# Two FNet and two H3 layers on one core: the 64-row products of rows 4 to 15 in runs of six over 384 columns, on three fixed banks

## The chip, the core and the metric

The kernel runs on one NeuronCore of a Trainium2 chip. TensorE (PE in the profile) multiplies matrices and writes the products to PSUM banks; PEld is its loading of weights. VectorE (DVE) and ScalarE (ACT) work element by element, GpSimd (POOL) does a few small steps and issues some transfers, SyncE (SP) issues most of the others. Each engine takes its instructions in order. The metric is the device time of one execution in microseconds, as the median of several runs.

## The reference

x has 2048 positions of 576 channels. Two layers alternate, twice:

```
x = x + FNet(layernorm(x));  x = x + H3(layernorm(x))
FNet(x) = Cr @ (x @ Wr.T) - Ci @ (x @ Wi.T)        # real part of a 2-D Fourier transform
H3(q)   = q * (longconv(kv, ssm_k) + kv * ssm_D),  kv = shiftconv(k, shift_k) * v
```

The shift convolution has 4 taps, the long one is causal over all 2048 positions; the reference does it by a transform of length 4096. k, v and the filters are inputs and do not depend on x, so this branch can be computed at any time before the first H3 layer needs it.

## The kernel before

A matrix product in fp32 accuracy is made of three: each operand is split into a high part (ScalarE rounds it, `split`, L92) and a low part (VectorE subtracts, L93), and TensorE adds high x high, high x low and low x high in one bank.

`layer` computes the sequence transform of a FNet layer. Its steps (g, tb, k) run over the real and the imaginary matrix (g), four blocks of 512 output positions (tb) and 16 blocks of 128 positions to sum over (k). A step has 14 products of 512 columns, 12 into four banks `s` and two into the bank `rm` for the last 64 channels; the left operand is X (tile `mats`), the right a 128 x 512 block of the matrix that `load_c` loads two steps ahead and splits. These are the "sequence products" below. After each block of positions `hidden` makes the transform over channels, 27 products of 288 columns into a bank `bk`.

`branch` is a generator that computes the convolution branch between these steps; the main loop calls it a fixed number of times in each step, so the sequence products set its pace. Its first part, f1, takes the 16 rows j of the input as (position in groups of 16) and transforms each over 128 entries by two transforms of 64. `todo` lists the pieces (j, src), src 1 for the filter (kernel) and 0 for the signal: first the filters of rows 0 to 3, then their signals, then both of each row from 4 on.

- `f1_loads` loads the piece and the row's constants, `convolve` makes the shift convolution on VectorE in small steps, paced so that a row's signal is ready when its piece comes up.
- `f1_split` multiplies in v for a signal and splits the piece into one of three buffers `xf`.
- `f1_products` takes a piece of 576 columns in two halves of 288. For each half it takes two banks from `bank()` (one tag with three buffers) and makes six products: for each of the three combinations of high and low one on partitions 0 to 63 and one on 64 to 127, which use a 64-row half of TensorE each and go to different banks. ScalarE copies both banks out (L436) and issues the store to `t_d` (L437), of which there is one for each column half.
- A piece's products are made one piece after its split, from the ninth piece on (`F1_LAG`) two pieces after.

Which instruction stands where on an engine is decided by a scheduler: it keeps the dependencies and the order that `issue_after` (here the helper `behind`) demands, and is otherwise free, so that the products of f1 are laid between the sequence products, six together or fewer.

After f1 comes the middle part: it reads `t_d` in groups of four frequencies (`load_feed`, L569), transforms, multiplies filter and signal and transforms back; its products stand between later sequence products and go to `bank()` too. Then the result is gated with x, and the second half of the kernel repeats the two layers with the filters' result kept.

Of the kernel before, what the change touches and what calls it, by code (L numbers as in the profile page):

```python
# [10 lines left out]
F32 = mybir.dt.float32  # L11
FR = mybir.dt.float32r
AF = mybir.ActivationFunctionType
OP = mybir.AluOpType

P = 128
HP = P // 2
S = 2048
D = 576
J = S // P  # L20
TB = 4
NT = 512
HD = D // 2
NC = 4
# [5 lines left out]
ROWS = (0, 1, 2, 3, 4, 5, 6, 7, 8, 9)  # L30
K_FIRST = 4
F1_16 = 5
F1_LAG = 8
F1_END = 42
W_FROM = 41
HOLD = 125
# [16 lines left out]
CRAW = 2  # L53
# [6 lines left out]
SC_AT = 8 + 4 * STAT  # L60
# [5 lines left out]
def fnet_h3_kernel(ctx: ExitStack, tc: tile.TileContext, x, c_mat, w_re, w_im, k_pad, v, shift_k,  # L66
                   ssm_k, ssm_d, f1c, i2c, midc, out):
    nc = tc.nc
    cst = ctx.enter_context(tc.tile_pool(name="cst", bufs=1))
    sb = ctx.enter_context(tc.tile_pool(name="sb", bufs=1))  # L70
    psp = ctx.enter_context(tc.tile_pool(name="psp", bufs=1, space=bass.MemoryType.PSUM))
    dr = ctx.enter_context(tc.tile_pool(name="dr", bufs=1, space=bass.MemoryType.DRAM))

    def mm(ps, lhsT, rhs, first, last, more=False):
        nc.tensor.matmul(ps, lhsT, rhs, start=first, stop=last, skip_group_check=more)  # L75

    def bank():
        return psp.tile([P, NT], F32, tag="b", bufs=3, name="bk")

    acc4 = [psp.tile([P, NT], F32, tag=f"s{i}", name=f"s{i}") for i in range(4)]  # L80
    last_pair = [acc4[2:]]
# [9 lines left out]
    def split(h, l, src):  # L91
        a = nc.scalar.activation(h, src, AF.Copy).ins  # L92
        return a, nc.vector.tensor_tensor(l, src, h.bitcast(F32), OP.subtract).ins  # L93

    @contextmanager
    def behind(*instructions):
        with ExitStack() as stack:
            for i in instructions:
                stack.enter_context(tc.issue_after(i))
            yield  # L100
# [22 lines left out]
    ring = {}  # L123

    def lay(t, at, *sizes):

        for name, words, n in sizes:
            ring.setdefault(name, Ring()).tiles.extend(t[:, at + i * words:at + (i + 1) * words] for i in range(n))
            at += n * words
        assert at <= t.shape[1], (at, t.shape, sizes)  # L130
        return at
# [5 lines left out]
    def two(v):  # L137
        return v.rearrange("p (a n) -> p a n", a=2)
# [11 lines left out]
    flts = flat(FLT, F32, "flts")  # L150
# [5 lines left out]
    anchor, made, rounded, pows, biased, halved, added, evac, parted, stored = [], [], [], [], [], [], [], [], [], []  # L156
# [35 lines left out]
        made.append(nc.vector.tensor_tensor(t[:, D + REM:], y[:, :NC * P], h[:, :NC * P], OP.subtract).ins)  # L192
        return t

    t_d = [dr.tile([P, 2 * J, 2, HD], F32, name=f"t{h}") for h in range(2)]
    v_d = [dr.tile([P, J, 2, HD], F32, name=f"vd{h}") for h in range(2)]
    yb_d = [dr.tile([P, D], F32, name=f"yb{j}") for j in range(J)]
    xa_d = [dr.tile([P, D], F32, name=f"xa{j}") for j in range(J)]
# [46 lines left out]
        load_after(xs[:, ch].bitcast(F32), w_d[ch])  # L245
        W[ch] = two(xs[:, ch])

    U = {}

    def ut(ch):  # L250
        return um[0][:, ch * WIDE:(ch + 1) * WIDE].rearrange("p (a n) -> p a n", a=2)
# [42 lines left out]
    def layer(get_x, xres, done, pending, blocks=TB):  # L294
        steps = [(g, tb, k) for tb in range(blocks) for g in range(2) for k in range(J)]
        for n, (g, tb, k) in enumerate(steps):
            for i in range(2):
                if n == 0 and steps[i] not in CT:
                    load_c(steps[i])
            if n + 2 < len(steps):  # L300
                load_c(steps[n + 2])
            for i in range(XLEAD + 1 if blocks == TB else 1):
                if n + i < J:
                    get_x(n + i)
            if k == 0:
                ps = list(acc4)
                ps.append(psp.tile([P, NT], F32, tag="rm", name="rm"))
            c = CT.pop(steps[n])
            first, last = k == 0, k == J - 1
            while last and g == 0 and pending:  # L310
                yield n, None
            for dc in range(NC):
                xh = X[k][:, dc * P:(dc + 1) * P]
                xl = X[k][:, D + REM + dc * P:D + REM + (dc + 1) * P]
                mm(ps[dc], xh, c[0], first, False)
                mm(ps[dc], xh, c[1], False, False)
                mm(ps[dc], xl, c[0], False, last)
                if dc == NC // 2 - 1:
                    yield n, False
                elif blocks == TB and dc < NC - 1 and n >= MID_FROM and not last:  # L320
                    yield n, "part"
                if last:
                    (evac_u if blocks == TB else save_u)(g, ps, dc)
            xr = X[k][:, NC * P:D + REM]
            mm(ps[NC], xr, c[0], first, False)
            mm(ps[NC], xr, c[1], False, last)
            if last and blocks < TB:
                store_r(tb, g, ps[NC])
            elif last:
                evac_r(g, ps)  # L330
                if g == 1:
                    us = dict(U)
                    pending.extend([us, tb, jj, xres, done] for jj in range(TB))
            yield n, True

    def parts(i):
        v = ring[i]()
        return v[:, :D], v[:, D:]
# [3 lines left out]

    def branch():
        f1r = region_b(FR, "f1r")
        lay(f1r, 0, ("xf", 2 * D, 3), ("fc", 2 * P, 5))
        at = lay(flts, SC_AT + CRAW * NT, ("so", D, 4), ("land", D, 3))
        lay(flts, at, ("craw", NT, 1))
        f1f = region_a(F32, "f1f")
        ks = f1f[:, :KR * 2 * D]
        lay(f1f, KR * 2 * D, ("wt", 2 * D, 2), ("rp", 2 * D, 2))  # L350
        tmp = f1f[:, 8 * 2 * D:]
        wt, rows, landed, fcs = [], {}, {}, {}
        k_loaded = [0]

        def load_w4():
# [20 lines left out]
        def convolve():  # L376
            for i in range(J // 2):
                if not wt:
                    load_w4()
                load_k(i + KR - 1)  # L380
                rp = rows[i] = two(ring["rp"]())
                for t in range(4):
                    out_t = two(tmp) if t else rp
                    for n, k in k_rows(2 * i + t):
                        nc.vector.tensor_tensor(out_t[:, n], k, wt[3 - t][:, n], OP.mult)
                    yield
                    if t == 1:
                        load_k(i + KR)
                    if t:
                        nc.vector.tensor_tensor(rp, rp, out_t, OP.add)  # L390
                        yield
# [22 lines left out]
        def f1_split(j, src):  # L414
            r = landed.pop((j, src))
            if not src:
                row = rows[j // 2][:, j % 2, :]
                nc.vector.tensor_tensor(row, row, r, OP.mult)
                r = row
            elif j == 0:  # L420
                nc.vector.tensor_tensor(r[:1], r[:1], tmp[:1, D:], OP.add)
            xf = parts("xf")
            parted[:] = split(xf[0], xf[1], r)
            return xf

        def f1_products(j, src, xf, fc):
            for hf in range(2):
                so = two(ring["so"]())
                cs = slice(hf * HD, (hf + 1) * HD)
                ps = [bank() for _ in range(2)]  # L430
                for n, (a, b) in enumerate(((0, 0), (0, 1), (1, 0))):
                    for i in range(2):
                        rows = slice(i * HP, (i + 1) * HP)
                        mm(ps[i][:, :HD], fc[rows, a, :], xf[b][rows, cs], n == 0, n == 2)
                for i in range(2):
                    stored[:] = [nc.scalar.activation(so[:, i, :], ps[i][:, :HD], AF.Copy).ins]  # L436
                nc.scalar.dma_start(t_d[hf][:, j::J, src, :], so)  # L437
                yield

        conv, made_ops, split_up = convolve(), 0, []  # L440
        for n, (j, src) in enumerate(todo):
            f1_loads(n + 1)
            if n < 2:
                yield
            split_up.append((j, src, f1_split(j, src), fcs[j]))
            products = f1_products(*split_up.pop(0)) if len(split_up) > (1 if n < F1_LAG else 2) else iter(())
            if n:
                f1_loads(n + 3)
            later = [m for m in range(n + 1, len(todo)) if todo[m][1] == 0 and 7 * (todo[m][0] // 2 + 1) > made_ops]
            for half in range(2):  # L450
                next(products, 0)
                if later and n > 2:
                    left = 7 * (todo[later[0]][0] // 2 + 1) - made_ops
                    for _ in range(-(-left // (2 * (later[0] - n) - half)) if left > 0 else 0):
                        next(conv)
                        made_ops += 1
                yield
        next(conv, 0)
        for left_over in split_up:
            yield from f1_products(*left_over)  # L460
        m1 = region_b(FR, "mid")
        kk_at = SC_AT + CRAW * NT + 4 * D
        at = lay(m1, 0, ("df", 2 * D, 3), ("mc", 4 * P, 1))
# [88 lines left out]
        def load_feed(i):  # L552
            if i < len(feeds):
                kind, hf, q = feeds[i]
                landed[i] = ring["land"]()
                load_after(landed[i], v_d[hf][:, q].rearrange("p c d -> p (c d)") if kind else
                           t_d[hf][4 * q:4 * q + 4].rearrange("m j s d -> (m j) (s d)"))

        def load_fc(k):
            if k < len(rows):  # L560
# [189 lines left out]
    for n, whole in layer(get_x0, lambda j: x[:, j, :], done0, pending):  # L750
# [30 lines left out]
        m = n - PREP  # L781
# [355 lines left out]
```

## Time and profile before

| | |
|---|---|
| median of 3 runs | 1210.28 us (1209.79 to 1210.68) |
| the profiled execution | 1208.79 us |
| its span, first to last instruction | 1207.0 us |
| busy: PE, PEld, DVE | 1189.2, 1004.4, 840.7 us |
| busy: ACT, POOL | 664.1, 76.2 us |
| bytes moved | 259.85 MB, mean 215 GB/s |

Busy times are unions of the time in which an engine has an instruction at work. TensorE's matmuls are pipelined: the next starts before the one before has ended, so a busy TensorE can still go faster, and its costs are better read from one start to the next. In a row of the timeline stand the start, the duration of the merged group, the engine, the line, the tiles written and read, the shape (rows x columns of the array, then partitions x elements) and the count. In a row of the waits stand who waited, for whom, the sum in us, the number of times and the longest. In a row of a windows view stand the stretch, its length and each engine's busy time with its number of instructions, then the granted clock, the DMA engines' busy share and the rate.

### The profile page before, as it was taken

Reading aid. Unit: us, or ns where it says so; the run is one execution under the profiler, and the core shown is the slowest. Engines: PE = TensorE matmul, PEld = TensorE weight load, DVE = VectorE, ACT = ScalarE, POOL = GpSimd, SP = SyncE. Lnnn points to the kernel's source line nnn. Section 1 sums busy time; section 2 is a strip of 40 time slices with the busy share of each in tenths; the row PEclk is TensorE's granted clock in tenths of the full one; section 3 lists DMA queues with packets and bytes.
Section 4 is the critical chain, followed back from the end, with each engine's and each line's share of the span. In section 5 each row is a group of like instructions: output and inputs, shape, how many; then the busy total and the mean of one; then the engine's idle time right before and its main releaser. Section 6 shows DMA issues by size and latency. Waiting matters only on the chain.

```text
span 1207.0 us, 18256 instructions
## 1 busy us (share of the span) xinstructions
PE 1189.2 (99%) x6320; PEld 1004.4 (83%) x6320; DVE 840.7 (70%) x1498; ACT 664.1 (55%) x1335; POOL 76.2 (6%) x116
## 2 busy tenths in 40 slices
PE   8999999999999999999999999999999999999997
PEld 5776667998888888888988898888888888789997
DVE  7889983678787677775346666775766777774764
ACT  7855555578876677775345667544434445450210
POOL 2210000000000000001101111000000000001111
PEclk9999999999999999999999999999999999999999
DMA  9768877645666666547967677872672677795621
GB/s 337 271 206 282 280 240 249 211 149 164 204 195 201 226 178 204 182 147 231 323 189 236 233 246 225 279 253 83 196 279 92 194 281 269 239 322 160 219 93 40
DMA packets 146110, 259.85 MB, mean 215 GB/s; under 512 B 15841, under 2 KB 46817, under 8 KB 146018
## 3 DMA queue, kind: packets, MB, share of 16 engines
q1 hardware_dynamic: 102674, 205.45, 52.3%
q10 hardware_dynamic: 36432, 42.63, 10.3%
q0 software_dynamic: 6912, 10.62, 3.4%
q8 instruction: 49, 0.80, 0.3%
q14 instruction: 43, 0.35, 0.1%
HBM read 191.99 MB, written 66.65 MB: 214 GB/s over the span
## 4 chain that ended last, share of the span: by engine, by line
PE 72%; ACT 4%; DVE 2%; DMA 2%; issue 1%; ACTq 0%; SPq 0%; POOLq 0%; DVEq 0%
PE s L75 39%; PE bk L75 29%; PE rm L75 4%; ACT flts L490 2%; ACT mid L490 1%; DMA wd<-w 1%; DMA t<-ud 1%; DMA flts<-in_c_mat 1%; ACT mats L92 0%; ACT u L92 0%; DVE mid L496 0%; DVE mats L93 0%; DVE flts L511 0%; DVE flts L509 0%; DVE flts L510 0%
## 5 line engine op out<-in xcount | busy, mean ns | idle before, releaser
L75 PE MATMUL s<-mats 128*128 128x512 f32 x2088 | 545.1, 396 | 0.6 <-DVE u L93 0.5
L75 PEld LDWEIGHTS s<-mats 128*128 128x128 f32 x2088 | 379.5, 188 | 81.2 <-issue 10.8
L93 DVE TENSOR_TENSOR mats<-flts,mats 128x512 fp32r<-128x512 f32 x206 | 140.9, 688 | 65.9 <-ACT mats L92 64.5
L92 ACT ACTIVATE mats<-flts 128x512 fp32r<-128x512 f32 x206 | 128.5, 628 | 86.3 <-PE bk L75 34.0
L75 PE MATMUL bk<-mid 128*128 128x288 f32 x768 | 132.5, 299 | 2.3 <-ACT flts L490 2.0
L75 PEld LDWEIGHTS bk<-mid 128*128 128x128 f32 x768 | 116.2, 188 | 21.8 <-ACT flts L490 8.1
L75 PE MATMUL bk<-w,u 128*128 128x288 f32 x864 | 120.6, 295 | 0.3 <-ACT flts L490 0.3
L75 PEld LDWEIGHTS bk<-w,u 128*128 128x128 f32 x864 | 117.3, 188 | 3.8 <-ACT flts L490 1.9
L496 DVE TENSOR_TENSOR mid<-flts,mid 128x576 fp32r<-128x576 f32 (+1 forms) x149 | 93.5, 628 | 35.3 <-ACT mid L490 32.7
L490 ACT ACTIVATE flts<-bk 128x288 f32<-128x288 f32 x160 | 62.1, 405 | 89.5 <-PE bk L75 77.1
L75 PE MATMUL rm<-mats 128*128 128x512 f32 x304 | 94.7, 391 | 0.0
L490 ACT ACTIVATE flts<-flts 64x288 f32<-64x288 f32 x192 | 85.0, 443 | 5.6
L490 ACT ACTIVATE mid<-flts 128x576 fp32r<-128x576 f32 (+1 forms) x148 | 80.4, 575 | 6.1 <-DMA flts<-t 2.9
L436 ACT ACTIVATE flts<-bk 128x288 f32<-128x288 f32 x128 | 46.9, 408 | 58.7 <-PE bk L75 58.6
L281 DVE TENSOR_TENSOR flts<-flts,bk 128x288 f32<-128x288 f32 x48 | 21.8, 453 | 67.3 <-PE bk L75 67.3
L75 PE MATMUL bk<-mats 128*128 128x288 f32 (+1 forms) x376 | 67.8, 317 | 0.0
L75 PEld LDWEIGHTS rm<-mats 128*128 128x128 f32 x304 | 56.9, 188 | 12.2 <-DVE flts L267 0.3
L75 PE MATMUL s<-t,mats 128*128 128x512 f32 x264 | 65.2, 390 | 0.3 <-DVE t L93 0.3
L75 PEld LDWEIGHTS bk<-f1r 64*128 64x128 f32 x384 | 34.9, 188 | 33.2 <-issue 15.2
L178 POOL TENSOR_TENSOR flts<-flts 128x1 f32<-128x1 f32 x35 | 28.6, 818 | 523.8 <-DVE flts L177 523.8
L75 PE MATMUL bk<-mats,t 128*128 128x288 f32 (+1 forms) x368 | 59.3, 303 | 0.0
L75 PE MATMUL bk<-f1r 64*128 64x288 f32 x384 | 53.3, 333 | 5.9 <-ACT f1r L408 5.7
(145 smaller groups left out, 1507.6 us busy)
## 6 DMA issues: line engine op xcount, KB each, us to landing
flts<-in_c_mat SPq DMA_DIRECT2D x148, 256.0 KB, 3.5
ph<-in_c_mat SPq DMA_DIRECT2D x54, 512.0 KB, 3.9
t<-flts ACTq DMA_DIRECT2D x64, 288.0 KB, 4.0
flts<-in_c_mat SPq DMA_DIRECT2D x30, 512.0 KB, 5.4
flts<-t SPq DMA_DIRECT2D x53, 288.0 KB, 2.9
vd<-flts ACTq DMA_DIRECT2D x64, 144.0 KB, 2.3
flts<-vd SPq DMA_DIRECT2D x32, 288.0 KB, 4.5
mid<-in_i2c POOLq DMA_DIRECT2D x32, 256.0 KB, 5.0
```

Of the source, the lines that this page charges most:

```text
L75: nc.tensor.matmul(ps, lhsT, rhs, start=first, stop=last, skip_group_check=more)
L92: a = nc.scalar.activation(h, src, AF.Copy).ins
L93: return a, nc.vector.tensor_tensor(l, src, h.bitcast(F32), OP.subtract).ins
L178: pows.append(nc.gpsimd.tensor_tensor(rs, ve, mhalf, OP.pow).ins)
L281: added[:] = [nc.vector.tensor_tensor(r[:, cs], r[:, cs], ps[:, :HD], OP.add).ins]
L436: stored[:] = [nc.scalar.activation(so[:, i, :], ps[i][:, :HD], AF.Copy).ins]
L490: last_act.append(nc.scalar.activation(*args, **kw).ins)
L496: nc.vector.tensor_tensor(l, src, h.bitcast(F32), OP.subtract)
```

## The change

- `bank()` gives three fixed tiles in turn in place of buffers of one tag.
- Rows 0 to 3 keep runs of six products over 288 columns. Their order in a run is now the upper half first, and high x low first. The buffers `xf` are four in place of three.
- From row 4 on (`K_FIRST`) the parts of signal and filter of one row are put side by side into one of two buffers `xp`, ordered (column half, source, 288), so that a row has 1152 columns, and three runs of six products take 384 (`VW`) columns each. The copies go to `sp`, three buffers in the place of `so`.
- `behind(*last)` puts the first product of a run behind the last sequence product (`seq`) recorded so far, and each further one behind the one before.
- The runs no longer belong to a piece's two halves of its turn; `visits` holds them with the earliest half turn each may take, and a half turn makes at most one run. Rows 0 to 3 are due one piece after their split, rows from 4 on three half turns after the start of their second piece.
- `t_d` is one tensor with all 1152 columns of a row, and the middle part reads its column halves.

The core of the diff:

```diff
+    banks, given = [psp.tile([P, NT], F32, tag=f"b{i}", name=f"bk{i}") for i in range(3)], [0]
     def bank():
-        return psp.tile([P, NT], F32, tag="b", bufs=3, name="bk")
+        given[0] += 1
+        return banks[(given[0] - 1) % 3]
...
-    t_d = [dr.tile([P, 2 * J, 2, HD], F32, name=f"t{h}") for h in range(2)]
+    t_d = dr.tile([P, 2 * J, 2 * D], F32, name="td")
...
-                mm(ps[dc], xl, c[0], False, last)
+                seq[:] = [mm(ps[dc], xl, c[0], False, last)]
...
-            mm(ps[NC], xr, c[1], False, last)
+            seq[:] = [mm(ps[NC], xr, c[1], False, last)]
...
-        lay(f1r, 0, ("xf", 2 * D, 3), ("fc", 2 * P, 5))
+        lay(f1r, 0, ("xf", 2 * D, 4), ("fc", 2 * P, 5))
+        lay(f1r, 0, ("xp", 4 * D, 2))
+        lay(flts, SC_AT + CRAW * NT, ("sp", 2 * VW, 3))
...
-            xf = parts("xf")
-            parted[:] = split(xf[0], xf[1], r)
-            return xf
+            if j < K_FIRST:
+                xf = parts("xf")
+                parted[:] = split(xf[0], xf[1], r)
+                return xf
+            if not src:
+                t = ring["xp"]()
+                paired[:] = t[:, :2 * D], t[:, 2 * D:]
+            h, l = (t.rearrange("p (a s d) -> p a s d", a=2, s=2)[:, :, src, :] for t in paired)
+            parted[:] = split(h, l, two(r))
+            return tuple(paired)
-        def f1_products(j, src, xf, fc):
...
+        def f1_products(j, fc, xf, at, n, so, to):
+            ps = [bank()[:, :n] for _ in range(2)]
+            last = seq[-1:]
+            for k, (a, b) in enumerate(((0, 1), (0, 0), (1, 0))):
+                for i in (1, 0):
+                    half = slice(i * HP, (i + 1) * HP)
+                    with behind(*last):
+                        last = [mm(ps[i], fc[half, a, :], xf[b][half, at:at + n], k == 0, k == 2)]
+            so = two(ring[so]())
+            for i in range(2):
+                stored[:] = [nc.scalar.activation(so[:, i, :], ps[i], AF.Copy).ins]
+            nc.scalar.dma_start(t_d[:, j::J, to:to + n], so)
...
+        def visit(half):
+            if visits and visits[0][0] <= half:
+                f1_products(*visits.pop(0)[1:])
...
-            split_up.append((j, src, f1_split(j, src), fcs[j]))
-            products = f1_products(*split_up.pop(0)) if len(split_up) > (1 if n < F1_LAG else 2) else iter(())
+            xf = f1_split(j, src)
+            if j < K_FIRST:
+                visits += [(2 * n + 2, j, fcs[j], xf, hf * HD, HD, "so", hf * D + src * HD) for hf in range(2)]
+            elif src:
+                visits += [(2 * n + 3, j, fcs[j], xf, at, VW, "sp", at) for at in range(0, 2 * D, VW)]
...
-                           t_d[hf][4 * q:4 * q + 4].rearrange("m j s d -> (m j) (s d)"))
+                           t_d[4 * q:4 * q + 4, :, hf * D:(hf + 1) * D].rearrange("m j d -> (m j) d"))
```

More of the change, by code (lines that the diff above doesn't have):

```diff
@@ L32 @@
 F1_16 = 5
-F1_LAG = 8
+VW = 384
 F1_END = 42
@@ L74, in mm @@
     def mm(ps, lhsT, rhs, first, last, more=False):
-        nc.tensor.matmul(ps, lhsT, rhs, start=first, stop=last, skip_group_check=more)
+        return nc.tensor.matmul(ps, lhsT, rhs, start=first, stop=last, skip_group_check=more).ins
+    banks, given = [psp.tile([P, NT], F32, tag=f"b{i}", name=f"bk{i}") for i in range(3)], [0]
     def bank():
-        return psp.tile([P, NT], F32, tag="b", bufs=3, name="bk")
+        given[0] += 1
+        return banks[(given[0] - 1) % 3]
     acc4 = [psp.tile([P, NT], F32, tag=f"s{i}", name=f"s{i}") for i in range(4)]
@@ L246, in reload_w @@
         W[ch] = two(xs[:, ch])
-    U = {}
+    U, seq = {}, []
     def ut(ch):
@@ L351, in branch @@
         tmp = f1f[:, 8 * 2 * D:]
-        wt, rows, landed, fcs = [], {}, {}, {}
+        wt, rows, landed, fcs, paired = [], {}, {}, {}, []
         k_loaded = [0]
@@ L421, in f1_split @@
                 nc.vector.tensor_tensor(r[:1], r[:1], tmp[:1, D:], OP.add)
-            xf = parts("xf")
-            parted[:] = split(xf[0], xf[1], r)
-            return xf
-        def f1_products(j, src, xf, fc):
[L427 to L440, printed above, removed]
+            if j < K_FIRST:
[20 more added lines that the diff above has]
+            nc.scalar.dma_start(t_d[:, j::J, to:to + n], so)
+        conv, made_ops, visits = convolve(), 0, []
+        def visit(half):
+            if visits and visits[0][0] <= half:
+                f1_products(*visits.pop(0)[1:])
         for n, (j, src) in enumerate(todo):
@@ L450, in branch @@
             for half in range(2):
-                next(products, 0)
+                visit(2 * n + half)
                 if later and n > 2:
@@ L458, in branch @@
         next(conv, 0)
-        for left_over in split_up:
-            yield from f1_products(*left_over)
+        for half in range(2 * len(todo), 2 * len(todo) + 4):
+            visit(half)
+            yield
         m1 = region_b(FR, "mid")
```

## The prediction

> **What bounds the kernel now.** I read the page's engine shares and slices first, then the windows view of the stretch in which the edited step (the 64-row products, tile f1r) runs, then TensorE's timeline inside it, then VectorE's waits.
>
> ```profile
> span 1207.0 us, 18256 instructions
> PE 1189.2 (99%) x6320; PEld 1004.4 (83%) x6320; DVE 840.7 (70%) x1498; ACT 664.1 (55%) x1335; POOL 76.2 (6%) x116
> PE   8999999999999999999999999999999999999997
> ```
>
> TensorE is busy in every slice, so what shortens its instruction stream can shorten the span, if nothing else becomes late. The edited products start at 5.7 us and end at 209 us:
>
> ```profile
> L75 PE MATMUL bk<-f1r x384: 285/292/607, 5.7 to 208.9; 64*128 64x288 f32 x192
> ```
>
> I cut their time at 15 us (start-up over) and at 99 us, where by the program order the changed kernel goes over to 384 columns (after 302 sequence products).
>
> ```profile
> core 0: us, PE busy (x) PEld busy (x) DVE busy (x) ACT busy (x) POOL busy (x), PEclk, DMA share, GB/s
> 15.00:99.00 84.00, 84.00 (x383) 61.44 (x382) 73.48 (x139) 60.02 (x126) 15.55 (x18) 1.00 0.79 267
> 99.00:209.00 110.00, 109.79 (x576) 75.76 (x575) 84.17 (x99) 62.44 (x145) 3.69 (x7) 1.00 0.83 261
> ```
>
> TensorE is full in both windows, at a granted clock of 1.00, and VectorE is at 87% in the first. The same windows by tile count TensorE's instructions: of the sequence products (tile mats) 289 and 300, of the 64-row products (tile f1r) 94 and 276.
>
> ```profile
> 15.00:99.00 84.00, 72.72 (x289) 1.00 0.79 267
> 99.00:209.00 110.00, 81.72 (x300) 1.00 0.83 261
> ...
> 15.00:99.00 84.00, 14.72 (x94) 1.00 0.79 267
> 99.00:209.00 110.00, 34.72 (x276) 1.00 0.83 261
> ```
>
> Busy times overlap there, so I price by start times from TensorE's timeline (start, duration, engine, what, count):
>
> ```profile
> 48.22 2.88 PE L75 MATMUL s<-mats 128*128 128x512 f32 x12
> 50.94 0.61 PE L75 MATMUL rm<-mats 128*128 128x512 f32 x2
> ...
> 168.37 0.66 PE L75 MATMUL bk<-f1r 64*128 64x288 f32 x3
> 168.96 0.50 PE L75 MATMUL s<-mats 128*128 128x512 f32 x1
> 169.39 0.66 PE L75 MATMUL bk<-f1r 64*128 64x288 f32 x3
> ...
> 178.43 0.66 PE L75 MATMUL bk<-f1r 64*128 64x288 f32 x6
> 179.03 1.65 PE L75 MATMUL s<-mats 128*128 128x512 f32 x6
> 180.61 0.66 PE L75 MATMUL bk<-f1r 64*128 64x288 f32 x6
> 181.20 1.66 PE L75 MATMUL s<-mats 128*128 128x512 f32 x6
> 182.69 0.62 PE L75 MATMUL rm<-mats 128*128 128x512 f32 x2
> 183.24 0.66 PE L75 MATMUL bk<-f1r 64*128 64x288 f32 x6
> ...
> 221.90 3.71 PE L75 MATMUL bk<-w,u 128*128 128x288 f32 x27
> 225.44 0.44 PE L75 MATMUL bk<-mid 128*128 128x288 f32 x2
> ```
>
> - A sequence product takes (50.94 - 48.22)/12 = 0.227 us.
> - From 178.43 to 183.24 stand two runs of six and 14 sequence products: 4.81 - 14 x 0.227 = 1.63, so a run of six costs 0.815 us with its entry and exit.
> - From 168.37 to 169.39 stand a run of three and one sequence product: 1.02 - 0.227 = 0.79 us. **Half a run costs as much as a whole one**: its three products, all of one row half, stand in a row, where in a run of six the two row halves run side by side.
>
> So the 64-row products cost now: first window 84.0 - 289 x 0.227 = 18.4 us for 94 (15.7 sixes, 1.17 us each); second 110.0 - 300 x 0.227 = 41.9 us for 276 (46 sixes, 0.91 each). A whole run would be 0.815; the rest is broken runs.
>
> **The change part by part.**
>
> *Whole runs.* In the order in which the built programs stand, the runs of before have lengths 1 to 12 (39 of 75 are sixes, 20 are threes); the changed one has 16 runs of six at 288 columns and 36 at 384, no other. Two of the 16 stand ahead of 15 us, 14 in the first window: 14 x 0.815 = 11.4 us.
>
> *384 columns.* Three runs do the work of four, the columns streamed stay the same. The 27 full-height products of 288 columns from 221.90 to 225.44 took 0.131 us each, those of 512 took 0.227, so 96 columns more are 0.041 us; three pairs to a run: +0.12, a run costs 0.935 (ends: 0.815, were it all entry and exit; 1.10 with the 0.096 us of a 512-column product per pair; I take the interpolated value, both ends being measured sizes). 36 x 0.935 = 33.7 us.
>
> *TensorE's sum alone:* first window 18.4 - 11.4 = 7.0 us less, second 41.9 - 33.7 = 8.2 less, 15.2 together.
>
> *What is late next: VectorE.* Its program is the same in amount and, but for small exchanges, in order. All its idle time in the first window is accounted for by these waits:
>
> ```profile
> DVE flts L653 <- POOL flts L631: 3.8, 7, 0.7
> DVE f1r L93 <- ACT f1r L92: 1.8, 1, 1.8
> DVE u L93 <- ACT u L92: 1.6, 2, 0.9
> DVE mats L191 <- ACT mats L189: 1.4, 3, 0.7
> DVE flts L630 <- ACT early L629: 0.7, 2, 0.5
> DVE flts L184 <- POOL flts L178: 0.7, 1, 0.7
> DVE mats L93 <- ACT mats L92: 0.4, 1, 0.4
> ```
>
> They sum to 10.4; 73.5 + 10.4 = 83.9 of 84.0 us. Most are inside the row statistics, which the change leaves alone. What follows TensorE or ScalarE's queue (1.8 of f1r, 1.6 of u) can shrink: I give it 3.0 us. The sequence products of this window need VectorE's low parts, so **the first window saves 3.0 us, not 7.0** (ends 0 and 7.0).
>
> In the second window VectorE has slack on the whole (84.17 of 110), but not at its front:
>
> ```profile
> 96.60:131.10 34.50, 32.09 (x36) 1.00 0.94 296
> ...
> 165.10:198.00 32.90, 19.66 (x24) 1.00 0.78 253
> ...
> 96.60:131.10 34.50, 6.01 (x8) 1.00 0.94 296
> ...
> DVE f1r L93 <- ACT f1r L92: 2.4, 1, 2.4
> ```
>
> Busy and its one wait of 2.4 us fill those 34.5 us (32.09 + 2.4). It split 8 tiles in them (third row), four pairs: 8.6 us for a pair. From 165 us on it is busy for only 60%. Changed TensorE needs for a pair (24 or 25 sequence products between the first runs of two pairs) 25 x 0.227 + 3 x 0.935 = 8.5 us. So the two go level, and I take off 1.0 us of TensorE waiting (ends 0 and 5). The second window saves 7.2 us.
>
> *Buffers.* A buffer now holds kernel and signal of a row, high and low parts (xp, two of them). The split into a buffer waits for the third run of the pair two before; behind it on ScalarE stand evacuations and the next sequence split, and VectorE's low part waits for it. Before, three buffers (xf) gave the same kind of wait, the 2.4 above. It is in the 1.0.
>
> *Splits* of rows 4 on write 2 x 288 columns with a stride in place of 576. Same counts:
>
> ```profile
> L436 ACT ACTIVATE flts<-bk 128x288 f32<-128x288 f32 x128 | 46.9, 408 | 58.7 <-PE bk L75 58.6
> L92 ACT ACTIVATE f1r<-f1f 128x576 fp32r<-128x576 f32 x16 | 10.9, 681 | 1.7 <-DVE f1f L418 1.6
> ...
> L93 DVE TENSOR_TENSOR f1r<-f1f,f1r 128x576 fp32r<-128x576 f32 x16 | 12.1, 753 | 6.4 <-ACT f1r L92 6.3
> ```
>
> Taken as equal; the upper end is two instructions of 288 on ScalarE, 816 against 681 ns, 24 x 0.135 = 3.2 us, and on VectorE I suppose no more than as much again, which would be bought from its front stretch; a gain is excluded, the elements being the same.
>
> *Evacuations* fall from 128 to 104; one of 384 columns is 408 + 96 x (681 - 408)/288 = 499 ns. ScalarE's sum falls from 52.2 to 32 x 0.408 + 72 x 0.499 = 49.0 us. It is not the bound (62 of 110 us busy): worth nothing.
>
> *DMAs.* Stores on ScalarE's queue fall from 64 to 52 with the same bytes; the 53 and more loads that read them back move as many bytes from one tensor in place of two.
>
> ```profile
> t<-flts ACTq DMA_DIRECT2D x64, 288.0 KB, 4.0
> ...
> flts<-t SPq DMA_DIRECT2D x53, 288.0 KB, 2.9
> ```
>
> The first read needs all stores. Last store and first read take 6.9 us together; between the last run and the first middle product stand 52 sequence products and 27 others (was 56 and 27): 11.8 + 3.5 = 15.3 us, which hides them. The rows' order of loads on SP's and POOL's queues stays. Start-up (before 15 us): one run fewer ahead of it, and the first steps wait for VectorE anyway: 0 (ends -1 and +1).
>
> **Sum.** 3.0 + 7.2 = 10.2 us. The profiled execution took 1208.79 us, 1.8 around its span of 1207.0; it would go to 1198.6 (span 1196.8). The median of the three runs, 1210.28, lies 1.5 above it: **1200.1**.
>
> **Rivals.**
> 1. *VectorE gives way*: its order is only as late as TensorE lets it be. Then the full 15.2 us are saved: 1195.1. For it: the waits of 1.8 and 2.4 us are on ScalarE's queue, which TensorE's earlier runs would free. Against it: of the first window's 10.4 us of waits 8.6 are others, and they stay.
> 2. *VectorE holds on to its waits*: front stretch and splits keep it level to the last rows, the second window saves 3: 1204.3. For it the full 34.5 us above; against it the 60% from 165 us on.
> 3. *Evacuation binds.* Three banks in turn, two to a run: the first bank of a run is the first one evacuated of the run before. Between runs six sequence products apart TensorE has 1.6 us; an evacuation needs 0.5 and, where a split stands ahead of it on ScalarE, 0.68 more. Every run held by 0.2 us gives 36 x 0.2 = 7.2: 1207.3. Against it: ScalarE waited for TensorE (58.6 us in the row above), not the other way. [...]
> 4. *Other side: the row halves lose their overlap.* The changed runs begin with the upper half (partitions 64 on). If a pair that starts so runs one after the other, each pair adds 0.131 + 0.041 us: 36 x 3 x 0.172 = 18.6 us in the second window, and of 14 x 0.39 = 5.5 in the first 1.5 beyond what VectorE hides; with no VectorE waits left 1200.1 + 18.6 + 1.5 - 1.0 = 1219. It decides from 55% of the pairs on (10.2 / 18.6). For it: before begins with the lower half; against it: the halves share nothing but VectorE's and ScalarE's outputs.
>
> **How the numbers follow.** Likeliest case 0.50, rival 1 0.17, rival 2 0.16, rival 3 0.10, rival 4 0.05, something unseen and slower 0.02. A measurement of this kernel tells about 0.2% (2.4 us) from no change, so rival 3 splits: 0.06 faster, 0.03 within, 0.01 slower. Faster 0.88, within 0.04, slower 0.08. The range goes from rival 1 less the start-up's microsecond to rival 3: 1194 to 1207.5; the likeliest case alone spans 1197 to 1203.
>
> **What would show it.** Products of f1r: 216 of 64x384 and 96 of 64x288, all in sixes, a run of 384 at 0.935 us beside 0.227 for a sequence product; evacuations x104. The 302nd sequence product near 96 us (99 now), the last run's end near 199 us. TensorE idle or low parts just in time up to about 130 us, free of it after. Wrong, if pairs show starts 0.17 us apart (rival 4), if runs wait on ScalarE's evacuation (rival 3), or if the 998 us behind 209 us, which I leave as they are, change by more than 2 us.

## The result and the profile after

The changed kernel takes 1198.2 us (median of 4 runs, 1197.14 to 1199.58), the one before 1210.13 in the same comparison: ratio 0.9902, 95% interval 0.9884 to 0.9919, so 11.9 us less. Forecast were 1200.1 us, 1194 to 1207.5. The profiled execution is the slowest of the four, 1199.58 us; that of the kernel before, 1208.79, is faster than the four runs compared here (1209.79 to 1210.68). So the two profiles differ by only 9.2 us.

The page of the changed kernel (span, and busy time with share and instructions by engine), and the tile view of its 64-row products (count, durations, first and last start):

```profile
span 1197.8 us, 18057 instructions
PE 1175.3 (98%) x6248; PEld 996.6 (83%) x6248; DVE 839.2 (70%) x1498; ACT 660.5 (55%) x1311; POOL 75.1 (6%) x116
...
L75 PE MATMUL bk<-f1r x312: 286/333/606, 6.6 to 198.1; 64*128 64x384 f32 x108, 64*128 64x288 f32 x48
```

TensorE runs 72 products fewer, and the last of the 64-row products starts at 198.1 us where it started at 208.9. (The form counts at the end of that row are of a sample of every second one.)

TensorE's timeline after, at the first run of 384 columns, in the steady part, and at the last run:

```profile
94.47 0.79 PE L75 MATMUL bk<-f1r 64*128 64x384 f32 x6
...
154.54 0.79 PE L75 MATMUL bk<-f1r 64*128 64x384 f32 x6
155.26 1.66 PE L75 MATMUL s<-mats 128*128 128x512 f32 x6
156.84 0.79 PE L75 MATMUL bk<-f1r 64*128 64x384 f32 x6
...
197.63 0.80 PE L75 MATMUL bk<-f1r 64*128 64x384 f32 x6
198.35 2.08 PE L75 MATMUL s<-mats 128*128 128x512 f32 x8
```

From 154.54 to 156.84 stand one run and six sequence products: 2.30 - 6 x 0.227 = 0.94 us for a run of 384. The first of them comes at 94.5 us, behind 302 sequence products, and the last run ends at 198.35 us, behind 606. Before, counted in the same way, 303 were done at 99.07 and so 302 some 0.3 us (a run's entry and one product) ahead of that, at 98.7; its last run ended at 209.08 us, behind 602. The rows of its timeline:

```profile
99.07 0.66 PE L75 MATMUL bk<-f1r 64*128 64x288 f32 x6
...
209.08 3.00 PE L75 MATMUL s<-mats 128*128 128x512 f32 x12
```

The windows of the changed kernel up to and from there, and who made VectorE (first window) and TensorE (from 11.15 to 198 us) wait:

```profile
15.00:94.50 79.50, 78.56 (x378) 59.48 (x377) 71.28 (x136) 58.52 (x121) 14.54 (x17) 1.00 0.82 269
94.50:198.30 103.80, 103.09 (x521) 71.27 (x520) 84.98 (x101) 60.37 (x124) 3.70 (x7) 1.00 0.89 286
```

```profile
DVE flts L672 <- POOL flts L650: 4.1, 7, 0.7
DVE flts L649 <- ACT early L648: 1.5, 3, 0.7
DVE mats L96 <- ACT mats L95: 1.0, 2, 0.5
DVE u L96 <- ACT u L95: 0.7, 1, 0.7
DVE mats L194 <- ACT mats L192: 0.5, 1, 0.5
DVE flts L647 <- ACT early L646: 0.4, 1, 0.4
...
PE bk L75 <- ACT flts L448: 0.9, 2, 0.7
PE s L75 <- ACT mats L192: 0.8, 1, 0.8
```

VectorE is again busy or in one of these waits for the whole first window (71.3 + 8.2 of 79.5); its 1.8 us for ScalarE's split of a row (f1r) are gone. TensorE now waits too, 1.7 us in all, where before it did not.

The start-up took longer in this profile. The second step of sequence products, in the timeline before and then in the one after, begins 1.0 us later than it did:

```profile
15.01 3.01 PE L75 MATMUL s<-mats 128*128 128x512 f32 x12
...
16.02 2.91 PE L75 MATMUL s<-mats 128*128 128x512 f32 x12
```

This start differs between executions: in the six profiles e6 to e11 below, whose edits all act later, the same step begins between 14.8 and 16.1 us. So how much of the 1.0 us belongs to the change is not shown, and ends of the stretch in two profiles are compared below together with their starts.

Behind the 64-row products a part of the gain is lost. TensorE's timeline after, at the first channel products (27 of them, then the first product of the middle part; in brackets idle time and its releaser):

```profile
210.25 2.92 PE L75 MATMUL bk<-w,u 128*128 128x288 f32 x21
213.69 0.40 PE L75 MATMUL bk<-w,u 128*128 128x288 f32 x1 [0.52 <-ACT w L237]
214.48 0.93 PE L75 MATMUL bk<-w,u 128*128 128x288 f32 x5 [0.39 <-DVE w L238]
215.25 0.43 PE L75 MATMUL bk<-mid 128*128 128x288 f32 x2
```

The channel products start 11.65 us earlier than before (221.90), the middle part 10.2 us (225.44), for the 27 took 5.0 us in place of 3.5: the last of the channel matrices w are late. The rest of what is lost, down to the 9.2 us at the end, goes in the middle part that follows, where TensorE waits for evacuations as it did not in this part before; its waits from 240 to 260 us:

```profile
PE bk L75 <- ACT flts L509: 1.2, 4, 0.5
```

### The profile page after: what moved, and what is told of

Its sections match the earlier page's. It is cut to its first block, busy times and chain, and to the rows that moved or that the text cites. A ratio compares the mean times of both kernels' runs of the same rounds, so it can differ in the third digit from the quotient of the medians.

```text
span 1197.8 us, 18057 instructions
## 1 busy us (share of the span) xinstructions
PE 1175.3 (98%) x6248; PEld 996.6 (83%) x6248; DVE 839.2 (70%) x1498; ACT 660.5 (55%) x1311; POOL 75.1 (6%) x116
## 3 DMA queue, kind: packets, MB, share of 16 engines
q10 hardware_dynamic: 33168, 42.63, 10.2%
## 4 chain that ended last, share of the span: by engine, by line
PE 76%; ACT 2%; DVE 2%; DMA 1%; issue 1%; POOLq 0%; DVEq 0%; ACTq 0%
PE s L75 42%; PE bk L75 30%; PE rm L75 4%; ACT flts L509 1%; DMA flts<-in_c_mat 0%; ACT u L95 0%; ACT mid L509 0%; DVE u L96 0%; DVE mid L515 0%; DVE flts L529 0%; ACT mats L95 0%; DVE flts L530 0%; DMA xa<-flts 0%; DMA mid<-td 0%; DVE flts L528 0%
## 5 line engine op out<-in xcount | busy, mean ns | idle before, releaser
L75 PE MATMUL bk<-mid 128*128 128x288 f32 x768 | 135.5, 301 | 3.0 <-ACT flts L509 1.6
L509 ACT ACTIVATE flts<-bk 128x288 f32<-128x288 f32 x160 | 62.2, 404 | 88.8 <-PE bk L75 82.4
L448 ACT ACTIVATE flts<-bk 128x384 f32<-128x384 f32 (+1 forms) x104 | 43.1, 462 | 45.7 <-PE bk L75 45.6
L75 PEld LDWEIGHTS bk<-mats 128*128 128x128 f32 x376 | 55.6, 188 | 3.4
L75 PEld LDWEIGHTS s<-t,mats 128*128 128x128 f32 x264 | 49.4, 188 | 10.6 <-DVE t L96 0.4
```

The lines of the kernel that those rows point to most:

```text
L75: return nc.tensor.matmul(ps, lhsT, rhs, start=first, stop=last, skip_group_check=more).ins
L448: stored[:] = [nc.scalar.activation(so[:, i, :], ps[i], AF.Copy).ins]
L509: last_act.append(nc.scalar.activation(*args, **kw).ins)
```

## The experiments

**Width and wholeness apart.** All runs of 288 columns, so four to a row; whole as in the changed kernel.

```diff
-VW = 384
+VW = 288
-                visits += [(2 * n + 3, j, fcs[j], xf, at, VW, "sp", at) for at in range(0, 2 * D, VW)]
+                visits += [(2 * n + 2, j, fcs[j], xf, at, VW, "sp", at) for at in range(0, 2 * D, VW)]
```

> The changed kernel with 288 columns in every run (rows 4 to 15 in four runs in place of three, due one half turn earlier), all 64 runs whole. Theory (a run has a fixed price of entry and exit beside its columns): a run of 288 costs about 0.79 us with entry and exit, one of 384 about 0.915, so rows 4 to 15 cost 48 x 0.79 = 37.9 us in place of 36 x 0.915 = 32.9: 5.0 us slower than the changed kernel, about 1203, so that some 7 of the 12 us saved belong to whole runs alone. Rival (the width does nothing, only the order counts): 1198. Second rival (the width is all, the order nothing): 1210.

Measured: 1204.51 us (10 runs, 1202.67 to 1210.98), ratio to before 0.9966 [0.9952, 0.9979]; 6 to 7 us slower than the changed kernel. Both rivals fall. The spread is wide, and its profiled execution, the 1211, shows what the longest execution holds. TensorE's timeline, ScalarE's, and TensorE's windows of that execution:

```profile
97.58 1.08 PE L75 MATMUL bk<-f1r 64*128 64x288 f32 x6 [2.06 <-ACT flts L448]
98.60 1.65 PE L75 MATMUL s<-mats 128*128 128x512 f32 x3
```

```profile
96.55 0.68 ACT L95 ACTIVATE f1r<-flts 128x576 fp32r<-128x576 f32 x1 [4.58 <-DMA flts<-in_ssm_k]
97.14 0.69 ACT L448 ACTIVATE flts<-bk 128x288 f32<-128x288 f32 x2
...
171.74 0.71 ACT L448 ACTIVATE flts<-bk 128x288 f32<-128x288 f32 x2 [3.40 <-DMA td<-flts]
```

```profile
95.00:105.00 10.00, 7.94 (x32) 0.66 0.69 238
...
170.00:180.00 10.00, 8.16 (x32) 0.66 0.59 199
```

A split stands on ScalarE's queue and waits 4.6 us for its filter row to land; behind it stand two evacuations, and the next run needs one of their banks. TensorE waits 2.06 us, and its granted clock (the number behind the count) falls to 0.66 in these 10 us: three sequence products take 1.65 us (98.60), where e12 below has 1.43 for five. The second wait, 1.84 us, has another cause: there the evacuation itself waited for an earlier store to free its buffer. The waits are no part of a run's price, so the width is priced again below.

**The order taken away.** The products keep their new shapes, the scheduler may lay them as it likes.

```diff
-                    with behind(*last):
-                        last = [mm(ps[i], fc[half, a, :], xf[b][half, at:at + n], k == 0, k == 2)]
+                    mm(ps[i], fc[half, a, :], xf[b][half, at:at + n], k == 0, k == 2)
```

> The changed kernel without the order behind the sequence products: the scheduler may break runs again. In its program stand 61 runs; of those with 384 columns 28 are sixes, 13 threes, one nine. Theory (half a run costs as much as a whole one): 28 + 13 sixes and threes at 0.915 and about 1.4 for the nine, 38.9 us against 32.9 for 36 whole runs, and in the first window up to 1 us more, since VectorE sets its end: 1204 to 1205. Rival (fewer columns' worth of entries is all, order worth nothing): 1198.

Measured: 1205.77 us (10 runs, 1202.77 to 1206.91), ratio 0.9968 [0.9958, 0.9977]. The theory holds, though the time lies 0.8 us above the 1205 that it gave as its upper end. Its timeline has the broken runs:

```profile
162.82 0.78 PE L75 MATMUL bk<-f1r 64*128 64x384 f32 x3
163.53 1.43 PE L75 MATMUL s<-mats 128*128 128x512 f32 x5
164.80 0.61 PE L75 MATMUL rm<-mats 128*128 128x512 f32 x2
165.34 0.78 PE L75 MATMUL bk<-f1r 64*128 64x384 f32 x3
```

Half a run of 384 and seven sequence products take 2.52 us: 2.52 - 7 x 0.227 = 0.93 us for the half run, as much as a whole one (0.94). Without the order most of the change's gain is gone: 3.7 us are left (1209.45 to 1205.77 on this chip) of the 11.9.

**The banks.** The order stays, `bank()` is again one tag with three buffers.

```diff
-        given[0] += 1
-        return banks[(given[0] - 1) % 3]
+        return psp.tile([P, NT], F32, tag="b", bufs=3, name="bk")
```

> The changed kernel with bank() as before (one tag, three buffers in place of three fixed tiles in turn). In its program eight of the runs of 384 are broken into one and five, for the first of a run has another bank than the one evacuated first. Theory: each broken run pays a second entry and exit, 0.2 us, and its lone product, about 0.35 us: 8 x 0.55 = 4.4 us in the second window, little in the first: 1202. Rival (the banks' names are nothing): 1198.

Measured: 1200.68 us (4 runs, 1200.31 to 1200.91), 2.5 us above the changed kernel's 1198.2. Its timeline:

```profile
154.89 0.79 PE L75 MATMUL bk<-f1r 64*128 64x384 f32 x5
155.61 1.20 PE L75 MATMUL s<-mats 128*128 128x512 f32 x4
156.73 0.44 PE L75 MATMUL bk<-f1r 64*128 64x384 f32 x1
157.10 0.97 PE L75 MATMUL s<-mats 128*128 128x512 f32 x3
157.99 0.79 PE L75 MATMUL bk<-f1r 64*128 64x384 f32 x5
```

From 154.89 to 157.99: 3.10 - 7 x 0.227 = 1.51 us for a run broken into five and one, 0.57 more than whole. Eight of them make 4.6 us in TensorE's stream. The profile bears that out: the last 64-row product starts at 200.1 us, 2.0 later than in the changed kernel, though the second step of sequence products began 1.8 us earlier (14.20 and 16.02). At the end only 2.5 us arrived. In the profiles, from the first middle product to the end, the lag falls from 3.2 us (218.5 and 215.25) to 1.1 (1198.9 and 1197.8). In part that is TensorE's waits in the middle part. Here they are, from 225 to 270 us, where the changed kernel has the 1.2 us for evacuations shown above:

```profile
PE bk L75 <- ACT flts L507: 0.2, 1, 0.2
```

Every other form that was run has the fixed banks, and in each profile stand the same four waits, 1.2 us together; the kernel before, with one tag, has none of them. So the fixed banks cost time in the middle part, which shares `bank()`. No form was run that has them in f1 alone. In f1 they let the scheduler keep a run whole, since a run then begins in the bank that is evacuated first.

**Which half first.** The lower row half first, banks and evacuations exchanged with it.

```diff
-            ps = [bank()[:, :n] for _ in range(2)]
+            ps = [bank()[:, :n] for _ in range(2)][::-1]
...
-                for i in (1, 0):
+                for i in (0, 1):
...
-            for i in range(2):
+            for i in (1, 0):
                 stored[:] = [nc.scalar.activation(so[:, i, :], ps[i], AF.Copy).ins]
```

> The changed kernel with the lower row half first in a pair, and the two banks of a run and their evacuations exchanged to fit, so that the program keeps 52 whole runs. Theory (a pair runs side by side whichever half is first): 1198, within 1.5 us. Rival (a pair that starts with the upper half loses something): faster than the changed kernel by 2 us or more.

Measured: 1197.31 us (4 runs, 1196.82 to 1198.62), the same as the changed kernel. A pair overlaps whichever half begins: a whole run of 384 takes 0.79 us in its timeline as in the changed kernel's, and from 154.66 to 156.96 stand one run and six sequence products, so 0.94 us for the run. And the runs stay whole so long as the first half's bank is the one evacuated first; the prediction's rival 4 is out.

**VectorE relieved.** Two of the four taps are left out on VectorE.

```diff
-                    for n, k in k_rows(2 * i + t):
+                    for n, k in k_rows(2 * i + t) if t < 2 else ():
...
-                        nc.vector.tensor_tensor(rp, rp, out_t, OP.add)
+                        if t < 2:
+                            nc.vector.tensor_tensor(rp, rp, out_t, OP.add)
```

> The changed kernel with two of the four taps of the shift convolution left out on VectorE (four of its seven operations for a row pair; the output is another one). Theory (VectorE sets the end of the first window): with about half of VectorE's convolution work gone the 302nd sequence product comes earlier than the 94.5 us of the changed kernel, by the 0.9 us in which TensorE idled and up to 1 us more; the second window gains up to 1 us as well. Rival (TensorE's own stream sets the first window once its runs are whole): the 302nd sequence product within 0.5 us of 94.5 us.

Measured: one run, 1197.21 us; the profiled executions of the unchanged form took 1199.58 and, on this chip, 1198.72 (e8 below). The windows of this run:

```profile
15.00:94.50 79.50, 79.50 (x389) 60.47 (x388) 63.28 (x133) 62.54 (x128) 11.03 (x18) 1.00 0.87 292
94.50:198.30 103.80, 103.80 (x520) 72.43 (x519) 56.24 (x75) 59.42 (x124) 4.22 (x8) 1.00 0.84 275
```

In the first window VectorE is 8 us less busy, TensorE is never idle and has 11 products more done (389 against 378). In this program two runs of 384 stand ahead of the 302nd sequence product, so that product is no fair mark; the last 64-row product starts at 195.3 us, against 198.1 and 197.5. Of these 2.2 to 2.8 us, 0.5 were there at the start (the second step begins at 15.48 us, against 16.02 and 15.99). So VectorE costs the changed kernel about 1.8 to 2.3 us in this stretch. Whether they come through to the end is open: the one time lies within the spread of the unchanged form (1196.36 to 1199.58).

**What is given back behind the stretch.** In the order of SyncE's queue the first read of td stands ahead of three loads of channel matrices, and it waits for one of the last stores of the stretch (in the profile after SyncE waits 4.0 us there, and 0.7 at the second read). SyncE's timeline after, and the first read and the last of these loads in the one before:

```profile
202.58 0.34 SPq L165 DMA_DIRECT2D mid<-td  x1
203.02 0.37 SPq L229 DMA_DIRECT2D flts<-in_w_im  x1
...
206.90 0.43 SPq L229 DMA_DIRECT2D flts<-in_w_im  x1
```

```profile
213.78 0.33 SPq L162 DMA_DIRECT2D flts<-t  x1
...
216.82 0.42 SPq L226 DMA_DIRECT2D flts<-in_w_im  x1
```

Before, the read stood ahead of three such loads as well. But the last of them was issued 5.1 us ahead of the first channel product (216.82 and 221.90), now 3.35 us (206.90 and 210.25): the last run stands four sequence products later in the order (606 for 602), which is 0.9 us, and the rest goes in the queue between. One edit begins these loads a step earlier:

```diff
-W_FROM = 41
+W_FROM = 40
```

> The changed kernel with the loads of the channel matrices begun one step earlier (W_FROM 40 in place of 41), which puts three of them ahead of the first read of td on SP's queue. Theory (behind the 64-row products some of the time saved is given back, since SP waits with that read for the last store of td and the matrices come late: the first 27 channel products took 5.0 us in place of 3.5): they take 3.5 us again and 1 to 2 us come off the whole, 1196 to 1197. Rival (what is saved there is waited for later in the middle part, whose order is its own): 1198.

> The same, begun two steps earlier (W_FROM 39): all of the matrices ahead of the first read of td. Theory: as with one step or up to 0.5 us better. Rival: 1198, or slower, if the matrices' splits on VectorE and ScalarE now hold up the last rows' splits.

> The changed kernel itself on the same chip, to compare the two with: 1198, within 1.5 us.

> The edit of the matrices' loads alone once more, whose times (1196.1 to 1198.0) overlapped the changed kernel's (1196.4 to 1198.7). Theory: 1196 to 1197, the middle part behind the 64-row products starting on time. Rival: 1197.5 to 1198.

Measured: W_FROM 40 1196.94 us (4 runs, 1196.14 to 1198.01) and, again, 1195.95 (4 runs, 1194.93 to 1196.96); the changed kernel on the first of these chips 1197.38 (4 runs, 1196.36 to 1198.72). W_FROM 39 1199.69 (4 runs, 1199.15 to 1200.00); this form computes something else (it seems that the matrices take over the convolution's tiles before the last rows have used them), so its time tells only of the order. Its rival came true there: the matrices' splits stand ahead of two evacuations on ScalarE, and TensorE waits 1.82 us for them (last section). TensorE's timeline of the second run of W_FROM 40:

```profile
209.86 3.71 PE L75 MATMUL bk<-w,u 128*128 128x288 f32 x27
213.41 0.44 PE L75 MATMUL bk<-mid 128*128 128x288 f32 x2
```

The 27 take 3.55 us again. All eight runs of it have a median of 1196.2 us, the eight of the changed kernel 1198.0. But on the one chip where both were run they stand closer, 1196.94 and 1197.38, each at a ratio to before of 0.9895; and the other two ratios, 0.9890 [0.9876, 0.9905] for W_FROM 40 and 0.9902 [0.9884, 0.9919] for the changed kernel, overlap. Part of the lead in the profiles also comes from elsewhere: near 1046 us TensorE waits 1.1 us for VectorE in the changed kernel (0.9 in e8), 0.2 or less in the two profiles of W_FROM 40, and less than 0.2 in e9 too, which lacks this edit. So the edit does what it was made for at the channel products, and its worth at the end, 0.4 to 1.8 us by the medians, is not settled. It is the fastest form that was run.

**Splits behind evacuations.** The wait of TensorE near 97 us that cost 2.06 us in the form with 288 columns is there in the changed kernel too, 0.71 us in its profile, 0.08 in another profiled execution of it (e8), and 1.24 in the form with the lower half first (e4). The edit puts the split that waits for its row behind the evacuations:

```diff
-            parted[:] = split(h, l, two(r))
+            with behind(*stored):
+                parted[:] = split(h, l, two(r))
```

> The changed kernel with each split of rows 4 to 15 put behind the last evacuation recorded (on ScalarE). Theory (the wait of TensorE near 97 us, 0.1 to 1.2 us from execution to execution, comes of a split that stands ahead of two evacuations on ScalarE's queue and waits for its filter row to land): the wait is gone from the trace, and 0.1 to 1 us from the time, 1197. Rival (TensorE would wait for that row's split a little later anyway): the wait comes back at the row's first run, 1198.

> Both small edits, the matrices' loads one step earlier and the splits behind the evacuations. Theory: first 27 channel products in 3.5 us, no wait near 97 us, 1196. Rival (what is saved is waited for later): 1198.

> 288 columns in every run, with the splits behind the evacuations. In the profiled execution of 288 columns without that order TensorE waited 2.06 and 1.84 us for an evacuation, and its clock was 0.66 in the 10 us around each wait; that execution took 1211, the others 1202.7 to 1206.9. Theory (those waits come of splits ahead of the evacuations): neither wait nor clock loss, 1202 to 1203, and a price of 0.79 us for a run of 288 read in the clean trace. Rival: waits and a spread as before, 1204.5.

Measured: with 384 columns 1197.43 us (1196.75 to 1199.52), with W_FROM 40 besides 1198.51 (1197.08 to 1199.13), with 288 columns 1200.48 (1199.24 to 1203.86). In all three the wait near 97 us is gone from the profile; one of 0.37 us stands near 122 in the first two. With 384 columns that is worth nothing that the runs can tell: the last 64-row product starts at 196.5 us, 1.0 earlier than in e8, but the second step of sequence products had begun 1.1 us earlier too (14.93 and 15.99), and the channel products wait 1.3 us for their matrices. Both edits together are no better than the changed kernel, and here the theory misses: in its profile TensorE waits 0.7 us at the last run and 1.15 us at the first middle products. With 288 columns the edit brings 4.0 us, and in its profile the clock stays at 1.00; the second kind of wait, for an evacuation behind a store, is gone there too, which the edit alone does not explain:

```profile
95.00:105.00 10.00, 10.00 (x58) 1.00 0.90 270
...
160.23 0.66 PE L75 MATMUL bk<-f1r 64*128 64x288 f32 x6
160.82 1.43 PE L75 MATMUL s<-mats 128*128 128x512 f32 x5
162.19 0.66 PE L75 MATMUL bk<-f1r 64*128 64x288 f32 x6
```

A run of 288 costs 1.96 - 5 x 0.227 = 0.83 us there. Between 288 and 384 columns, both with this order, lie 3.0 us of time (1200.48 and 1197.43) and 4.6 us at the last 64-row product (201.1 and 196.5); by the prices it would be 48 x 0.83 - 36 x 0.94 = 6.0. Behind the stretch the difference shrinks from 4.6 to 2.9 at the first middle product (216.98 and 214.05), for the 27 channel products take 3.55 us with 288 columns and 5.4 with 384; why the stretch has 4.6 and not 6.0 stays open. Whole runs of 288 columns, with this order, thus take 8.8 us off the kernel before (1209.3 to 1200.5 on this chip), the width 3 more; without this order it was 4.9 (1209.45 to 1204.51) and 7 more.

## Why the prediction was right

The time was right, 1198.2 for 1200.1, and so was the mechanism: whole runs, at the price forecast, on a TensorE that stays full. That the sum came so near is partly luck. From profile to profile, forecast against measured, the start gave 0 and -1.0 us, the first window 3.0 and 5.2, the second 7.2 and 7.4, and what stands behind 0 and -2.4: together 10.2 and 9.2. The medians differ by more, 11.9, since the profiled execution lies at the low end of its runs before and at the high end after.

- **The price of a run.** Forecast 0.815 us for 288 columns and 0.935 for 384; measured 0.83 and 0.94. That half a run costs a whole one holds at 384 too (0.93).
- **First window.** Forecast 3.0 us less with ends 0 and 7.0; the 302nd sequence product came 4.2 us earlier (98.7 to 94.5), although the start, put at 0 with ends -1 and +1, lost 1.0 (15.01 to 16.02); the window itself gave 5.2. The reason given holds in part: VectorE is full or in its row statistics again. But the window is not VectorE's alone, as "the first window saves 3.0, not 7.0" had it: TensorE idles for only 0.9 of its 79.5 us, and relieving VectorE gave 1.8 to 2.3 us over both windows, where the prediction had set 5.0 (4.0 and 1.0). The term of VectorE was more than twice too large. The window took 79.5 us; TensorE's own sum, 77.0, the 0.9 of idle time and the 1.0 of the later start make 78.9, and 0.6 stay open.
- **Second window.** Forecast 7.2 us. From 98.7 to 209.08 it was 110.4 us for 300 sequence products, from 94.47 to 198.35 it is 103.9 for 304; 6.5 and four products (0.9) make 7.4. TensorE waited 0.7 us in it, where 1.0 had been set aside.
- **Behind it.** The prediction left the 998 us as they were, and said that the order of loads on SP's queue stays. This step failed, by the prediction's own mark of 2 us: up to the channel products 11.65 us were gained, and the profiled execution kept 9.2. I had counted the sequence products behind the last run (52 for 56) as cover for the store and its first read alone, and not for what is queued behind that read on SP, three loads of channel matrices that lost 1.7 us of their lead (5.1 to 3.35). The waits of 1.2 us in the middle part were not foreseen either. They come with the fixed banks: with `bank()` as before (e3) they are gone.
- **Evacuation (rival 3).** One of 384 columns took 489 ns, forecast 499; ScalarE as such did not become the limit (busy 60.4 of the second window's 103.8 us), and in the stretch no wait shows that the copies' length alone explains. The place was right all the same: one of TensorE's two waits of size in the stretch is for an evacuation, held up in ScalarE's queue by a split that waits 4.2 us for a DMA.
- **Rivals 1, 2 and 4.** The full 15.2 us did not come, nor did VectorE hold the second window; the row halves overlap in either order (e4).
- **Splits with a stride** were taken as equal: VectorE's low parts of this tile take 749 to 751 ns, before 753.

## What to carry to other kernels

Count what a mode of TensorE costs by the run, from start to start, not by the product: here three half-height products cost as much as six (0.93 and 0.94 us at 384 columns), because a lone row half has no partner. In the profile before, the three products of one row half (the run at 168.37 us) start over some 0.36 us; the three pairs of a whole run (178.43) start over 0.38, the two of a pair within 0.02 of each other. What a run costs beside its columns is paid either way; it is about 0.5 us, an estimate from the line through 0.83 us at 288 columns and 0.94 at 384. Whole runs were worth 8.8 us and the greater width 3.0 more, once the evacuations no longer stood behind a waiting split. To keep runs whole in a scheduler's hands, give the order and a turn of banks in which the next run begins in the bank that is emptied first, and look at what else draws on these banks. When a stretch of the bounding engine is shortened, look on the DMA queues for loads behind a read that waits for one of the stretch's last stores: here they took 1.5 us of the gain at once.

## What the runs showed of the hardware that was not expected

A wait of TensorE of about 2 us cost more than itself here. In the form with 288 columns waits of 2.06 and 1.84 us each came with slower products: the 10 us around each wait hold 32 products in 7.94 and 8.16 us of busy time, where the same stretches of e12 hold 58 and 56 in 10.00, and the granted clock is 0.66 over them, in e12 1.00. Against e12, the same form without the waits, the stretch ended 11.4 us later (201.1 and 212.5 for the last 64-row product). Of this 3.9 are the waits and 1.7 a later start-up, and what remains, near 6, fits the slow clock: (1 - 0.66) x 10 = 3.4 us for each wait. The times of that form go with the clock as well: its mean over an execution is 0.998 in the three runs of 1202.7 to 1203.5 us and 0.993 in the 1211. W_FROM 39 (e7) has a third such wait; its timeline, and a window of it:

```profile
187.29 0.97 PE L75 MATMUL bk<-f1r 64*128 64x384 f32 x6 [1.82 <-ACT flts L448]
...
188.00:190.00 2.00, 2.00 (x6) 0.50 1.00 324
```

A wait of 1.24 us at the first of these places in e4 left the clock at 1.00. Waits of 1.82, 1.84 and 2.06 us were followed by the low clock, in three places of two executions.
